# Infini-attention with a token-mixing MLP: packing the attention logits into 46 steps of seven PSUM banks

## The chip, the cores and the metric

The kernel runs on one core of a Trainium2 chip. The time is device time in microseconds (us), the median of several executions. TensorE (PE) does the matmuls into PSUM, which has eight banks of 512 fp32 columns in each of 128 partitions; ScalarE (ACT), VectorE (DVE) and GpSimd (POOL) work on what comes out of them; the queue of SyncE (SP) issues all DMAs. [...]

## The reference, cut to what matters

x has 2048 tokens of width 1024; there are 32 heads of width 32 and 4 segments of 512 tokens.

```python
xn = layernorm(x)
q, k, v = heads of xn @ wq, xn @ wk, xn @ wv          # (32 heads, 4 segments, 512, 32)
for s in range(4):
    logits = qs @ ks.T * 32 ** -0.5 + causal mask     # 512 x 512 for each head
    a_dot = softmax(logits) @ vs
    a_mem = (phi(qs) @ M) / (phi(qs) @ z + 1e-6)      # memory of the earlier segments
    o = g * a_mem + (1 - g) * a_dot                   # g = sigmoid(beta), by head
    M, z = M + phi(ks).T @ vs, z + sum(phi(ks))
h = layernorm(xn)
y = (gelu(h.T @ w1 + b1) @ w2 + b2).T                 # mixes tokens; 3584 hidden units
return x + concat(o) @ wo + y
```

phi(t) is t + 1 where t > 0 and exp(t) otherwise.

## The kernel before

**Stages.** In the first stage x is loaded and normalised, and the MLP's hidden layer is computed (`norm_and_first_hidden`, `hidden`): 896 matmuls of 512 columns into `gT`. In the second stage (`attention_and_out`) the attention runs, and between its parts stand the matmuls of the MLP's second layer with `w2h` and those of the output projection with `wo_sb`, which together are called the fill (`_Fill`). The last part of the output projection comes in `tail`.

**Units.** A unit is one segment of four heads: 32 units, numbered u = 8 x segment + group. Its q and k projections (`proj_q`, `proj_k`, eight matmuls each) give qT and kT, in which head r of the group holds partitions 32r to 32r + 31. Three buffers of each are in rotation, by u modulo 3. Two units make a pair p: A is unit 2p, B is unit 2p + 1.

**Logits.** A block (kb, r) of a unit is the product of head r's keys 128 kb to 128 kb + 127 with its queries from 128 kb to 511; queries before that are masked anyway. So it has 512, 384, 256 or 128 columns for kb = 0, 1, 2, 3. Its contraction runs over 32 rows, and `tile_position` puts it on row group r of TensorE's array, a strip of 32 rows. Blocks share banks: kb 1 with kb 3 of the same unit and head (384 + 128), kb 2 of A with kb 2 of B (256 + 256), and kb 0 alone. A pair thus fills 20 banks. `window` computes them in three windows of 7, 7 and 6 banks, of 10, 12 and 10 matmuls; the order in a window is a table, where A13 means unit A, kb 1, head 3:

```python
    WINDOWS = (
        "A00 A01 A02 A03 A10 A11 A12 A30 A31 A32",
        "A20 A21 A22 A13 B20 B21 B22 A33 B00 B01 A23 B23",
        "B10 B11 B02 B03 B30 B31 B12 B13 B32 B33",
    )
```

ACT takes the exp of each bank into one of 14 slots of `pT` (512 columns of bf16 each; `EXPS` and `place` fix which), and POOL zeroes the upper triangle of each diagonal block of 128 columns with an `affine_select`; `MASKS` groups these over slots, so that there are 11 selects for a pair.

**Products.** `weigh(u, qb)` multiplies the exps of the four heads, for 128 queries, with V (1280 matmuls of 33 columns in all), adds the memory's product with `pqT` and `MZbf` from the second segment on, and for qb = 3 the update with `pk`. `combine` divides and gates on DVE into `o_s`, and a transposing DMA puts that into `oT`.

**The order.** A planner in the program (`_Flow`) writes the order of all engines while the kernel is built. It keeps a modelled clock for each engine. TensorE's attention tasks wait in a list (`crit`); the planner takes one when its inputs and banks are ready in the model by 120 ns, otherwise it issues a fill matmul. `GOALS` says for each pair how many of the 1088 fill matmuls should be done by then, so the fill lasts until the end. A window or step is a `wall`: no task behind it is taken ahead of it. On the chip nothing is decided any more; the order stands. A window is priced in the model at 637 ns.

**Loads.** SP's queue issues the weights of wq and wk (two buffers each), the w2h blocks of seven matmuls (six buffers, two blocks ahead), x for the residual into one of three `stg` buffers, in which DVE adds the fill's result (line 1349), and the stores from there. At the end `tail` loads what was stored into `fin`, adds and stores it (line 1265).

Matmuls are recorded at line 217 and DMAs at line 245, both helpers'; exps of logits are line 1083, the selects line 1091, evictions of projections lines 987 and 988.

## Time and profile before

| | |
|---|---|
| median of 6 runs | 694.37 us (694.13 to 694.7) |
| the profiled execution's own time | 694.46 us |
| its span, first to last instruction | 692.5 us |
| TensorE (PE) busy | 688.0 us (99%), 4822 matmuls |
| ScalarE (ACT) busy | 281.9 us (41%), 513 instructions |
| VectorE (DVE) busy | 268.6 us (39%), 603 instructions |
| GpSimd (POOL) busy | 118.0 us (17%), 235 instructions |
| granted TensorE clock | 1.0 |
| DMA engines, mean over the span | 112 GB/s |

A busy share counts the time in which at least one instruction of the engine is under way. Matmuls overlap, and each is recorded with its way through the array and out, so a 512-column matmul shows 0.38 us although the next one starts earlier; the step from one start to the next is what it costs. PEld is the weight load, which runs beside the matmuls. In the timeline a row is a run of like instructions: start, length, engine, line, operation, output<-inputs, shape, count. In the chain of waits a row is start, length and what the end of the kernel was waiting for in that time.

### The profile page before, as it was taken

To read this page: it belongs to the slowest core of one execution; us is meant where nothing else is said; L and a number is where in the kernel's file an instruction comes from. 1 tells how busy PE (TensorE), PEld (TensorE's weight loads), DVE (VectorE), ACT (ScalarE), POOL (GpSimd) and SP (SyncE) were. 2 spreads that over 40 slices of the span, in tenths; PEclk is the share of its full clock that TensorE was granted. 3 is DMA by queue.
4 is the path that set the end of the run, shared out by engine and by line. 5 is a ranking of instruction groups with operands and counts; after the bars stand their busy time and mean duration, and the time that the engine had idled before them with its cause. 6 is when DMAs were issued, how large, how long until landed. Compare 5 with 4: busy or idle time off the path is not lost.

```text
span 692.5 us, 11588 instructions
## 1 busy us (share of the span) xinstructions
PE 688.0 (99%) x4822; PEld 329.0 (48%) x4822; DVE 268.6 (39%) x603; ACT 281.9 (41%) x513; POOL 118.0 (17%) x235
## 2 busy tenths in 40 slices
PE   8999999999999999999999999999999999999998
PEld 3444444444444544545445454444445454444544
DVE  6731100000002433434555464655556463453545
ACT  7431111111136364454544525354543525443450
POOL 4820000000001221221202112121212212121230
PEclk9999999999999999999999999999999999999999
DMA  8377666223038445446262643526263442424114
GB/s 306 122 183 181 153 157 212 88 61 101 1 106 186 103 94 133 103 109 137 46 147 63 134 96 81 124 52 147 53 145 82 94 110 53 116 57 117 38 26 147
DMA packets 211342, 77.32 MB, mean 112 GB/s; under 512 B 173915, under 2 KB 203611, under 8 KB 211291
## 3 DMA queue, kind: packets, MB, share of 16 engines
q1 hardware_dynamic: 211290, 76.59, 44.6%
q8 instruction: 38, 0.62, 0.4%
q14 instruction: 14, 0.11, 0.0%
HBM read 59.79 MB, written 5.24 MB: 94 GB/s over the span
## 4 chain that ended last, share of the span: by engine, by line
PE 98%; ACT 1%; DMA 0%; DVE 0%; POOL 0%; issue 0%; SPq 0%; DVEq 0%
PE ps_all L217 98%; ACT xn_tmp L806 0%; DMA xin<-in_A_x_dram 0%; ACT xn_tmp L808 0%; DVE h L847 0%; POOL ln_r L839 0%; SPq L245 0%; DVE fin L1265 0%; POOL ln_t L837 0%; DVE ln_mv L822 0%; DVEq L65 0%
## 5 line engine op out<-in xcount | busy, mean ns | idle before, releaser
L217 PE MATMUL ps_all<-gT,w2h 128*128 128x512 bf16 x896 | 229.0, 379 | 0.0
L1083 ACT ACTIVATE pT<-ps_all 128x512 bf16<-128x512 f32 x320 | 161.9, 617 | 111.3 <-PE ps_all L217 111.3
L217 PE MATMUL ps_all<-h,w1all 128*128 128x512 bf16 x896 | 193.9, 379 | 0.8 <-DVE h L847 0.6
L1091 POOL TENSOR_SCALAR_AFFINE_SELECT pT<-pT 128x256 bf16<-128x256 bf16 (+3 forms) x176 | 91.8, 527 | 544.3 <-ACT pT L1083 540.3
L217 PEld LDWEIGHTS ps_all<-h,w1all 128*128 128x128 bf16 x896 | 87.5, 98 | 107.2 <-issue 1.3
L217 PEld LDWEIGHTS ps_all<-gT,w2h 128*128 128x128 bf16 x896 | 79.9, 97 | 82.6 <-issue 7.8
L961 ACT ACTIVATE gT<-ps_all,bc 128x512 bf16<-128x512 f32 x56 | 37.7, 689 | 139.9 <-PE ps_all L217 139.9
L1129 DVE CAST ost<-ps_all 128x264 bf16<-128x264 f32 (+1 forms) x128 | 50.5, 397 | 80.4 <-PE ps_all L217 79.8
L217 PEld LDWEIGHTS ps_all<-vA,pT 128*128 128x128 bf16 x1280 | 50.3, 96 | 29.6 <-POOL pT L1091 0.5
L217 PE MATMUL ps_all<-xnT,wq 128*128 128x512 bf16 x256 | 60.5, 379 | 0.0
L217 PE MATMUL ps_all<-xnT,wk 128*128 128x512 bf16 x256 | 60.5, 379 | 0.0
L217 PE MATMUL ps_all<-wv_sb,xnT 128*128 128x512 bf16 x256 | 60.1, 379 | 0.0
L217 PE MATMUL ps_all<-vA,pT 128*128 128x33 bf16 x1280 | 51.7, 178 | 0.0
L988 DVE CAST qT<-ps_all 128x512 bf16<-128x512 f32 x29 | 20.1, 692 | 79.8 <-PE ps_all L217 79.8
L987 ACT ACTIVATE vA<-ps_all 128x512 bf16<-128x512 f32 x18 | 10.8, 599 | 90.6 <-PE ps_all L217 90.6
L899 DVE TENSOR_SCALAR gcol<-gcol 128x32 f32<-128x32 f32 x1 | 0.2, 181 | 118.5 <-ACT gcol L897 118.5
L217 PEld LDWEIGHTS ps_all<-wv_sb,xnT 128*128 128x128 bf16 x256 | 25.1, 98 | 30.2
L217 PEld LDWEIGHTS ps_all<-xnT,wk 128*128 128x128 bf16 x256 | 25.0, 98 | 30.2
L217 PEld LDWEIGHTS ps_all<-xnT,wq 128*128 128x128 bf16 x256 | 25.0, 98 | 30.1 <-issue 0.2
L987 ACT ACTIVATE kT<-ps_all 128x512 bf16<-128x512 f32 x32 | 19.1, 597 | 37.6 <-PE ps_all L217 37.6
L217 PE MATMUL ps_all<-wo_sb,oT 128*128 128x512 bf16 x128 | 34.3, 379 | 0.0
L972 DVE TENSOR_SCALAR etmp<-etmp 128x512 bf16<-128x512 bf16 x48 | 17.6, 367 | 39.0 <-ACT etmp L971 39.0
(68 smaller groups left out, 424.2 us busy)
## 6 DMA issues: line engine op xcount, KB each, us to landing
w2h<-in_B_w_dram SPq DMA_DIRECT2D x64, 224.0 KB, 3.3
w1all<-in_B_w_dram SPq DMA_DIRECT2D x12, 1024.0 KB, 5.3
wq<-in_A_wq_dram SPq DMA_DIRECT2D x32, 256.0 KB, 3.0
wk<-in_A_wk_dram SPq DMA_DIRECT2D x32, 256.0 KB, 2.9
stg<-in_A_x_dram SPq DMA_DIRECT2D x16, 256.0 KB, 3.6
out_dram<-stg SPq DMA_DIRECT2D x16, 256.0 KB, 3.1
xin<-in_A_x_dram SPq DMA_DIRECT2D x5, 512.0 KB, 7.3
wv_sb<-in_A_wv_dram SPq DMA_DIRECT2D x2, 1024.0 KB, 8.3
```

Source lines behind the costliest of these rows:

```text
L217: ins = self.nc.tensor.matmul(out, *args, **kwargs)
L899: fw.op("dve", lambda e: e.tensor_scalar(self.gcol[:], self.gcol[:], 1.0, None, op0=ALU.add), reads=[self.R_gcol], writes=[self.R_gcol])
L961: fw.op("act", lambda e: e.activation(self.gT[:, fc, half * 512:(half + 1) * 512], self.bank(b), ACT.Gelu_apprx_tanh, bias=self.b1c[:, fc: ...
L972: fl.op({"dve": (lambda e: e.tensor_scalar(et[:], et[:], 1.0, None, op0=ALU.min), 294, 330)}, [R_et], [R_et], prio=2)
L987: self.flow.op({"act": (lambda e, b: e.activation(dst, view(self.bank(b)), ACT.Copy), 635, 560), "dve": (lambda e, b: e.tensor_copy(dst, v ...
L988: "dve": (lambda e, b: e.tensor_copy(dst, view(self.bank(b))), 690, 727)},
L1083: fl.op({"act": (lambda e, b, slot=slot: e.activation(pT[:, slot, :], self.bank(b), ACT.Exp, scale=SCALE), 620, 530)}, [], [R[slot]], box= ...
L1091: fl.op({"pool": (lambda e, ap=ap, pat=pat: e.affine_select(ap, ap, pattern=pat, compare_op=ALU.is_ge, fill=0.0, base=0, channel_multiplie ...
L1129: fl.op({"dve": (lambda e, b: e.tensor_copy(dst, self.ps[:, b, 0:n * VW]), 150 + n * 35, 185 + n * 35)}, [], [self.R_ost[o][qb]], box=box, ...
```

## The change

The windows become steps. `logit_steps` lays the banks of each row group in one queue over all pairs: kb 0 of the first unit, its kb 1 with kb 3, kb 2 of both units, kb 0 of the second unit, its kb 1 with kb 3. A step takes one bank from each row group and a second bank from three of them; the one that is left out rotates (3, 2, 1, 0). That makes 45 steps of seven banks and a last one of five. `step` writes the matmuls bank by bank in that order. Each bank has its own slot of `pT`, taken from a free list of 18 and given back when the units in it have been weighed, and its own `affine_select` of one or two blocks, 320 in all. The loop of `attention_and_out` issues projections when a step two ahead needs them and weighs a unit once its last step is issued; the goals of the fill come from straight lines between points instead of the table. Beside that, `prod` becomes half as large (`combine` writes one half into `o_s` and adds the other), `etmp` has one buffer instead of two, `stg` two instead of three, and `o_s` moves to another place.

```diff
-    GOALS = (0, 0, 60, 119, 179, 238, 310, 382, 454, 526, 598, 670, 742, 814, 885, 956, 1026, 1085)
+    N_SLOT = 18
+    RESERVE = 60
...
-        self.prod = e.take("prod", [P, 32, D_HEAD], BF16)
-        self.R_prod = [Res(f"prod{k}", wait) for k in range(2)]
+        self.prod = e.take("prod", [P, 4, P], BF16)
+        self.R_prod = Res("prod", wait)
+        self.o_s = [e.take(f"o_s{i}", [P, 4, P], BF16) for i in range(2)]
+        self.R_os = [Res(f"o_s{i}", wait) for i in range(2)]
...
-        self.etmp = [e.take(f"etmp{i}", [P, SEG_L], BF16) for i in range(2)]
+        self.etmp = e.take("etmp", [P, SEG_L], BF16)
...
-        self.pT = e.take("pT", [P, 14, 512], BF16)
+        self.pT = e.take("pT", [P, self.N_SLOT, 512], BF16)
...
-        self.stg = [e.take(f"stg{i}", [P, D_MODEL], BF16) for i in range(3)]
+        self.stg = [e.take(f"stg{i}", [P, D_MODEL], BF16) for i in range(2)]
...
+        self.slots = deque(range(self.N_SLOT))
+        self.slot_of, self.users = {}, {}
...
-    def phi(self, dst, R_dst, src, R_src, k):
+    def phi(self, dst, R_dst, src, R_src):
 
         fl = self.flow
-        et, R_et = self.etmp[k], self.R_etmp[k]
+        et, R_et = self.etmp, self.R_etmp
...
-    def place(o, kb, qb, r):
-
-        j = qb - kb
-        if kb == 2:
-            return 8 + r, o * 256 + j * P
-        if o == 0:
-            return (r if kb == 0 else 4 + r), (384 if kb == 3 else j * P)
-        if kb == 0:
-            return (12 + r if r < 2 else r), j * P
-        return 4 + r, (384 if kb == 3 else j * P)
-
-    WINDOWS = (
-        "A00 A01 A02 A03 A10 A11 A12 A30 A31 A32",
-        "A20 A21 A22 A13 B20 B21 B22 A33 B00 B01 A23 B23",
-        "B10 B11 B02 B03 B30 B31 B12 B13 B32 B33",
-    )
-    EXPS = ((0, 1, 2, 3, 4, 5, 6), (7, 8, 9, 10, 11, 12, 13), (4, 5, 2, 3, 6, 7))
-    MASKS = (
-        ((0, 16, 4), (16, 28, 4), (19, 28, 4)),
-        ((28, 32, 3), (32, 48, 2), (48, 56, 4)),
-        ((16, 24, 4), (19, 24, 4), (8, 16, 4), (24, 32, 4), (27, 32, 4)),
-    )
-
-    def window(self, p, w):
+    def logit_steps():
+
+        todo = []
+        for r in range(4):
+            q = deque()
+            for p in range(N_UNIT // 2):
+                x, y = 2 * p, 2 * p + 1
+                for blocks in (((x, 0),), ((x, 1), (x, 3)), ((x, 2), (y, 2)), ((y, 0),), ((y, 1), (y, 3))):
+                    q.append((r, blocks))
+            todo.append(q)
+        steps = []
+        while any(todo):
+            n = len(steps)
+            take = [q.popleft() for q in todo if q]
+            for r in range(4):
+                if todo[r] and r != (3 - n) % 4:
+                    take.append(todo[r].popleft())
+            steps.append(take)
+        return steps
+
+    def step(self, items):
         fl = self.flow
-        slots = self.EXPS[w]
-        items = [("AB".index(t[0]), int(t[1]), int(t[2])) for t in self.WINDOWS[w].split()]
-        units = sorted({2 * p + o for o, _, _ in items})
-        reads = [R[u % 3] for u in units for R in (self.R_kT, self.R_qT)]
+        slots, jobs, reads = [], [], []
+        for r, blocks in items:
+            slot = self.slots.popleft()
+            slots.append(slot)
+            col, masks = 0, []
+            for u, kb in blocks:
+                self.slot_of[u, r, kb] = (slot, col)
+                jobs.append((len(slots) - 1, u, r, kb, col))
+                masks.append(col // P)
+                col += SEG_L - kb * P
+                for R in (self.R_kT[u % 3], self.R_qT[u % 3]):
+                    if R not in reads:
+                        reads.append(R)
+            self.users[slot] = {u for u, _ in blocks}
+            items[len(slots) - 1] = (r, blocks, slot, masks)
 
         def mms(*bs):
-            bank = dict(zip(slots, bs))
-            for o, kb, r in items:
-                k = (2 * p + o) % 3
-                slot, col = self.place(o, kb, kb, r)
-                n_q = SEG_L - kb * P
-                self.fw.mm(self.ps[:, bank[slot], col:col + n_q],
-                           self.kT[k][32 * r:32 * r + 32, kb * P:(kb + 1) * P],
-                           self.qT[k][32 * r:32 * r + 32, kb * P:SEG_L],
+            for i, u, r, kb, col in jobs:
+                self.fw.mm(self.ps[:, bs[i], col:col + SEG_L - kb * P],
+                           self.kT[u % 3][32 * r:32 * r + 32, kb * P:(kb + 1) * P],
+                           self.qT[u % 3][32 * r:32 * r + 32, kb * P:SEG_L],
                            start=True, stop=True, tile_position=(32 * r, 0))
 
         box = fl.pe(mms, reads, banks=len(slots), wall=True, ns=637)
         pT, R = self.pT, self.R_pT
-        for i, slot in enumerate(slots):
+        for i, (r, blocks, slot, masks) in enumerate(items):
             fl.op({"act": (lambda e, b, slot=slot: e.activation(pT[:, slot, :], self.bank(b), ACT.Exp, scale=SCALE),
                            620, 530)}, [], [R[slot]], box=box[i], give=True)
-        v = pT[:].rearrange("p a (j q) -> p (a j) q", q=P)
-        for b0, b1, st in self.MASKS[w]:
-            ap = v[:, b0:b1:st, :]
-            rs = [R[i] for i in sorted({x // 4 for x in range(b0, b1, st)})]
-            pat = [[0, ap.shape[1]], [1, P]]
-            ns = 180 + 115 * ap.shape[1]
+            v = pT[:, slot, :].rearrange("p (j q) -> p j q", q=P)
+            if len(masks) > 1:
+                ap, pat = v[:, masks[0]:masks[1] + 1:masks[1] - masks[0], :], [[0, 2], [1, P]]
+            else:
+                ap, pat = v[:, masks[0], :], [[1, P]]
+            ns = 180 + 115 * len(masks)
             fl.op({"pool": (lambda e, ap=ap, pat=pat: e.affine_select(ap, ap, pattern=pat, compare_op=ALU.is_ge,
                                                                       fill=0.0, base=0, channel_multiplier=-1),
-                            ns, ns + 30)}, rs, rs)
+                            ns, ns + 30)}, [R[slot]], [R[slot]])
...
-        where = {(r, kb): self.place(u % 2, kb, qb, r) for r in range(4) for kb in range(qb + 1)}
+        where = {}
+        for r in range(4):
+            for kb in range(qb + 1):
+                slot, col = self.slot_of[u, r, kb]
+                where[r, kb] = slot, col + (qb - kb) * P
...
-            for k in range(2):
+            for k, to, R_to in ((0, os, R_os), (1, self.prod, self.R_prod)):
                 v = ost[:].rearrange("p (q k r) x -> p q k r x", q=4, k=2)[:, :, k, :, 0:D_HEAD]
                 rk = rec.rearrange("p (q k r) -> p q k r", q=4, k=2)[:, :, k, :].unsqueeze(3)
-                pk = self.prod[:].rearrange("p (k q r) d -> p k q r d", q=4, k=2)[:, k]
+                pk = to[:].rearrange("p q (r d) -> p q r d", d=D_HEAD)
                 dve(lambda e, v=v, rk=rk, pk=pk: e.tensor_tensor(pk, v, rk.to_broadcast([P, 4, 4, D_HEAD]), op=ALU.mult),
-                    R_ost + [R_rec], [self.R_prod[k]], 640)
-            pv = self.prod[:].rearrange("p (k q r) d -> p k q (r d)", q=4, k=2)
-            dve(lambda e: e.tensor_tensor(os[:], pv[:, 0], pv[:, 1], op=ALU.add), self.R_prod, [R_os], 424)
+                    R_ost + [R_rec], [R_to], 640)
+            dve(lambda e: e.tensor_tensor(os[:], os[:], self.prod[:], op=ALU.add), [R_os, self.R_prod], [R_os], 424)
...
-        for p in range(N_UNIT // 2):
-            a, b = 2 * p, 2 * p + 1
-            fl.stage = p + 1
-            self.window(p, 0)
-            self.proj_q(a + 2)
-            self.proj_k(a + 2)
-            self.window(p, 1)
-            self.proj_v(a)
-            for qb in range(4):
-                self.weigh(a, qb)
-            self.combine(a)
-            self.window(p, 2)
-            self.proj_q(b + 2)
-            self.proj_k(b + 2)
-            for qb in range(4):
-                self.weigh(b, qb)
-            self.combine(b)
-            self.proj_v(b)
-        self.stall = fl.run(self.GOALS)
+        steps = self.logit_steps()
+        first, last = {}, {}
+        for i, items in enumerate(steps):
+            for _, blocks in items:
+                for u, _ in blocks:
+                    first.setdefault(u, i)
+                    last[u] = i
+        made, u = 2, 0
+        for i, items in enumerate(steps):
+            fl.stage = i + 1
+            self.step(items)
+            while True:
+                if made < N_UNIT and made < u + 3 and first[made] <= i + 2:
+                    self.proj_q(made)
+                    self.proj_k(made)
+                    made += 1
+                elif u < N_UNIT and last[u] <= i:
+                    self.proj_v(u)
+                    for qb in range(4):
+                        self.weigh(u, qb)
+                    self.combine(u)
+                    for slot in [x for x, us in self.users.items() if u in us]:
+                        self.users[slot].discard(u)
+                        if not self.users[slot]:
+                            del self.users[slot]
+                            self.slots.append(slot)
+                    u += 1
+                else:
+                    break
+        goals = [0, 0]
+        knots = [(0, 0)] + [(last[8 * s + 7] + 2, 245 + 288 * s) for s in range(3)]
+        knots += [(len(steps) - 1, self.fill.total - self.RESERVE), (len(steps), self.fill.total - 3)]
+        for i in range(1, len(steps) + 1):
+            (x0, y0), (x1, y1) = next((k0, k1) for k0, k1 in zip(knots, knots[1:]) if k0[0] <= i <= k1[0])
+            goals.append(y0 + (y1 - y0) * (i - x0) / (x1 - x0))
+        self.stall = fl.run(goals)
...
-                self.flow.dma(lambda: fw.dma(k.stg[m % 3][:], k.x_d[:, k.mlp_order[m], :], writes=[k.R_stg[m % 3]]),
-                              [], [k.R_stg[m % 3]]) if m < len(k.mlp_order) else None
+                self.flow.dma(lambda: fw.dma(k.stg[m % 2][:], k.x_d[:, k.mlp_order[m], :], writes=[k.R_stg[m % 2]]),
+                              [], [k.R_stg[m % 2]]) if m < len(k.mlp_order) else None
...
-            m = j % 3
+            m = j % 2
```

## The prediction

> **What bounds the kernel now.** I read the page first, then the chain of work that ended last, then the waits, then the timeline of TensorE around the instructions that the change touches.

> ```profile
> PE 688.0 (99%) x4822; PEld 329.0 (48%) x4822; DVE 268.6 (39%) x603; ACT 281.9 (41%) x513; POOL 118.0 (17%) x235
> ```

> TensorE is busy for 688.0 of 692.5 us, all others under half. Busy matmuls overlap, so that alone proves little. The chain of waits does:

> ```profile
> 12.38 660.89 PE ps_all L217 x4597
> 673.31 16.77 PE ps_all L217 x123
> 690.11 0.36 DVE fin L1265
> ```

> From 12.38 us to 690 us the chain is TensorE alone; the one break, before 673.31, is a wait of 0.2 us for the last masks. So no wait is left to win and any cover is nearly whole: time changes by what TensorE's own stream gains or loses, plus new waits. The timeline prices that stream:

> ```profile
> 322.60 1.89 PE L217 MATMUL ps_all<-wv_sb,xnT 128*128 128x512 bf16 x8
> 324.32 1.24 PE L217 MATMUL ps_all<-gT,w2h 128*128 128x512 bf16 x5
> 325.50 0.61 PE L217 MATMUL ps_all<-qT,kT 32*128 32x512 bf16 x10
> 326.04 1.25 PE L217 MATMUL ps_all<-gT,w2h 128*128 128x512 bf16 x5
> 327.13 1.89 PE L217 MATMUL ps_all<-xnT,wq 128*128 128x512 bf16 x8
> 328.86 0.59 PE L217 MATMUL ps_all<-gT,w2h 128*128 128x512 bf16 x2
> ```

> Take differences of starts, not durations. Eight full matmuls last 324.32 - 322.60 = 1.72 us, or 0.216 us each for 512 columns: 0.054 us for 128 columns, which I call one unit. The logits window lasts 326.04 - 325.50 = 0.54 us; the other two kinds of window, in the same view,

> ```profile
> 306.81 0.62 PE L217 MATMUL ps_all<-qT,kT 32*128 32x256 bf16 x12
> 307.36 1.25 PE L217 MATMUL ps_all<-gT,w2h 128*128 128x512 bf16 x5
> ...
> 313.02 0.61 PE L217 MATMUL ps_all<-qT,kT 32*128 32x384 bf16 x10
> 313.57 0.39 PE L217 MATMUL ps_all<-gT,w2h 128*128 128x512 bf16 x1
> ```

> last 0.55 us each. A window's matmuls use 32 rows, so four run side by side, one in each row group. The fullest row group of each window takes 1024 columns, 8 units or 0.43 us; 0.11 us is left for leaving the mode. Entering costs too: five full matmuls take 325.50 - 324.32 = 1.18 us where 5 x 0.216 = 1.08 would do, so 0.10 us. The view of the logits' matmuls alone, by stretches of that window, shows the side by side:

> ```profile
> 325.49:325.71 0.22, 0.21 (x4) 1.00 0.30 39
> 325.72:325.88 0.16, 0.16 (x7) 1.00 1.29 267
> ```

> For 0.22 us only four matmuls are there, one per row group; the fifth in order, for row group 0 again, appears once the first has streamed its 512 columns. A matmul whose row group is taken waits.

> **The change, part by part.**

> *Steps in place of windows.* The matmuls of the logits are the same 512, and all other matmuls keep their count in the built program (4,822). 48 windows become 46 steps. Column sums: each row group has 16 x 20 units of work, and the steps give no row group more than 8 units, so with perfect packing 46 x 8 = 368 units stand against 48 x 8 = 384. That is -16 x 0.054 = -0.86 us, and two entries and exits fewer are -2 x 0.21 = -0.42 us.

> But the order inside changes as well. A window was written group by group: 384 columns for row groups 0, 1, 2, and only then the 128 that share their banks. `step` writes bank by bank: a slot with blocks 1 and 3 gives 384 and then 128 columns to the *same* row group, next to each other; a slot of two blocks 2 gives 256 and 256. The second of a pair must wait for the first, by the stretch view above. What do the matmuls behind it do, which are for idle row groups? In the windows of before this never comes up: I walked all three by hand, and each matmul's row group comes free no later than its turn, so both answers give 8 units. The row that is nearest shows a wait but not what stands behind one.

> [...] I work out both.

> In order: a matmul starts at the later of (its row group free, the previous matmul's start). Example, the 13th step: row groups 0 to 3 with 3+1 units each, then 0 to 2 with 2+2. Group 0: 3 units at 0, 1 unit at 3. Group 1 can start only at 3: 3 units, then 1 at 6. Group 2 at 6, its 1 at 9. Group 3 at 9, its 1 at 12. Then group 0 takes 2 at 12 and 2 at 14, group 1 at 14 and 16, group 2 at 16 and 18: the end is 20 units, not 8. The pattern of slots repeats after 20 steps; their lengths in units are 14, 14, 17, 17, 12, 17, 17, 12, 16, 17, 11, 14, 20, 14, 13, 19, 14, 14, 16, 17, sum 305. 46 steps are two rounds and the first six again (the last step has five banks, also 17): 2 x 305 + 91 = 701 units. Against 384 units: +317 x 0.054 = +17.1 us. With the two entries and exits: +16.7 us.

> Independently: 368 units, -0.86 - 0.42 = -1.3 us.

> I take the first. [...]

> *Masks.* 176 selects become 320, one per slot: 192 of 256 columns and 128 of 128.

> ```profile
> L1091 POOL TENSOR_SCALAR_AFFINE_SELECT pT<-pT 128x256 bf16<-128x256 bf16 x112 | 48.1, 431 | 142.6 <-ACT pT L1083 139.7
> L1091 POOL TENSOR_SCALAR_AFFINE_SELECT pT<-pT 128x384 bf16<-128x384 bf16 x32 | 16.7, 522 | 14.4 <-ACT pT L1083 13.3
> ```

> A block of 128 costs 522 - 431 = 0.09 us more, so one alone is about 0.34 us. 192 x 0.431 + 128 x 0.34 = 126 us of POOL instead of 91.8, of a span of 690. What counts is the step: seven exps of a window take 3.54 us in the ACT timeline, 0.51 us apart, and a select takes 0.34 to 0.43, so POOL keeps up and ends less than 0.5 us after the last exp. The full matmuls that stand on TensorE between a step and the products that read it hide this; without that cover each step would pay up to 0.4 us, 46 x 0.4 = 18 us. From below, not grouping selects may remove the 0.2 us wait at 673, since the last step is now followed by 14 full matmuls (3.0 us). I take -0.2.

> *Exps, projections, combine.* 320 exps as before. Nine qT evictions move from DVE to ACT and six of vA the other way (692 ns and 597 ns for 512 columns): both engines stay under half busy, nothing. `combine` has the same number of operations; the sum now waits for `prod` and `o_s` as before. One `etmp` for two, so the k side's exp waits for the q side's last DVE pass, at most 0.63 + 0.37 + 0.70 us; pqT and pk are read by products that come at least a projection and many full matmuls later. Nothing; without cover, 24 times up to 1 us.

> *Slots and queue.* 18 slots only loosen waits. Two staging buffers instead of three: the load of a chunk of x now waits on SP's queue for the store of the previous chunk, and w2h, wq and wk loads stand behind it. Store to landing is 3.1 us. In the built order a w2h load and mostly a transpose of o_s, which waits for DVE, stand between store and load, and each chunk lasts about 30 us, so I take nothing. Upper end: 14 chunks x 3.1 us held, 43 us; unlikely.

> *Sum.* The profiled execution took 694.46 us (span 692.5), within 0.1 of the median 694.37. 694.4 + 17.1 - 0.4 - 0.2 = 710.9, said as 711.

> **Rivals.** (1) *Row groups run on independently*: a row group can hold the waiting half without stopping the queue. Even one waiting matmul per row group brings every step down to 8 units. Then 694.4 - 1.3 - 0.2 = 692.9 us, on the other side of no change. [...] The point of decision is whether group 1's 384 columns start beside group 0's 384 or with its 128. (2) *Weight loads add to it*: where a 54 ns block is followed by its row group's next one, that load (92 ns in the trace) is not covered; in the windows it was, and the measured 0.11 us exit leaves no room for more. At 46 steps x up to 0.1 us: 716 us. (3) *The products wait for masks or w2h*, with row groups independent: 692.9 plus about 0.2 us in each step, 702 us. Against: TensorE's chain has one wait today, and POOL is paced by ACT.

> **How the numbers follow.** In order, alone or with (2): 0.84. Independent: 0.13; at -1.5 us it lies on the edge of what a measurement of this kernel can tell (0.2%, 1.4 us), so I split it 0.07 faster and 0.06 the same. Waits (3): 0.03, slower. Slower is 0.84 + 0.03 = 0.87. The time is that of the in-order case. The range 704 to 716 holds that case with the fixed cost per step off by 0.1 us either way (46 x 0.1 = 4.6 us) and some half steps overlapping; that is about 0.8, so it need not reach the faster case.

> **What would show it.** Right: steps of 0.7 to 1.2 us from first logits matmul to the next full one, mean about 15.2 x 0.054 + 0.11 = 0.93 us, the longest every 20th from the 13th; TensorE still one unbroken chain; other rows at the same 0.216 us. Wrong by (1): every step 0.55 us. Wrong by (3): PEld or PE rows that wait for POOL's pT or for w2h.

## The result and the profile after

The changed kernel takes 692.93 us (median of 19 runs, 692.78 to 693.19) against 694.43 us for the old one in the same comparison: the ratio is 0.9978, with a 95% interval of 0.9972 to 0.9984. It is faster by 1.5 us, where the prediction said slower by 17 and left the time of its rival (1), 692.9 us, outside its range.

The page of the changed kernel, first row of engines:

```profile
PE 686.7 (99%) x4822; PEld 329.4 (48%) x4822; DVE 260.5 (38%) x600; ACT 284.0 (41%) x516; POOL 145.8 (21%) x379
```

TensorE has lost 1.3 us and is still the bound. The chain of waits, its last pieces (start, length, what):

```profile
12.39 676.43 PE ps_all L217 x4703
688.84 0.36 DVE fin L1292
```

The chain is now TensorE without any break from 12.39 us to the end: the wait of 0.2 us for the last masks, before 673.31 us in the old kernel, is gone, and nothing new has come. The first stage, which was not changed, takes the same time: the first fill matmul starts at 214.41 us in the old trace and at 214.42 in the new one. So the difference of the spans, 692.474 - 691.215 = 1.26 us, lies in TensorE's own stream behind that point. The times differ by 1.50 us. The other 0.24 us or so lies outside the spans, before the first or after the last instruction (694.46 - 692.47 = 1.99 us in the old kernel's profiled execution, 692.94 - 691.22 = 1.72 in the new one's); no run here explains it.

Here is the 13th step, for which the prediction worked out 20 units (1.08 us, and 0.11 us more at its end), in the timeline of TensorE:

```profile
322.02 1.46 PE L217 MATMUL ps_all<-gT,w2h 128*128 128x512 bf16 x6
323.41 0.62 PE L217 MATMUL ps_all<-qT,kT 32*128 32x384 bf16 x14
323.96 1.25 PE L217 MATMUL ps_all<-gT,w2h 128*128 128x512 bf16 x5
```

It lasts 323.96 - 323.41 = 0.55 us, like an old window, and so do all others: the 45 full steps and the last one take 541 to 559 ns by the starts in the trace, the 48 old windows 541 to 549. The view of the logits' matmuls alone, in stretches of that step (stretch, its length, PE's busy time, the number of matmuls that touch it; the last three figures, clock and DMA, play no part here), says how:

```profile
323.40:323.57 0.17, 0.16 (x4) 1.00 1.12 337
323.58:323.63 0.05, 0.05 (x8) 1.00 1.08 246
323.64:323.74 0.10, 0.10 (x11) 1.00 0.78 184
```

The program has 384, 128, 384, 128, 384, 128, 384, 128 columns here, for row groups 0, 0, 1, 1, 2, 2, 3, 3. In the first 0.17 us four matmuls are under way; the single starts in the trace are 4, 11, 17 and 24 ns after the step's first weight load, all 384 columns wide. The second instruction in the program, 128 columns for row group 0, starts at 177 ns. So three later instructions started ahead of it. That was the point of decision which the prediction named, and it fell the other way. It also corrects a sentence that stands at the beginning, that on the chip nothing is decided any more and the order stands: between row groups, TensorE's starts in this trace do not keep the order of the program (11, 17 and 24 ns ahead of 177).

### The profile page after: what moved, and what is told of

The parts are those of the page before. It is cut to its first block, busy times and chain, and to the rows that moved or that the text cites. A ratio compares the mean times of both kernels' runs of the same rounds, so it can differ in the third digit from the quotient of the medians.

```text
span 691.2 us, 11771 instructions
## 1 busy us (share of the span) xinstructions
PE 686.7 (99%) x4822; PEld 329.4 (48%) x4822; DVE 260.5 (38%) x600; ACT 284.0 (41%) x516; POOL 145.8 (21%) x379
## 4 chain that ended last, share of the span: by engine, by line
PE 98%; ACT 1%; DMA 0%; DVE 0%; POOL 0%; issue 0%; SPq 0%; DVEq 0%
PE ps_all L217 98%; ACT xn_tmp L809 0%; DMA xin<-in_A_x_dram 0%; ACT xn_tmp L811 0%; DVE h L850 0%; POOL ln_r L842 0%; SPq L245 0%; DVE fin L1292 0%; POOL ln_t L840 0%; DVE ln_mv L825 0%; DVEq L65 0%
## 5 line engine op out<-in xcount | busy, mean ns | idle before, releaser
L217 PE MATMUL ps_all<-gT,w2h 128*128 128x512 bf16 x896 | 228.5, 379 | 0.0
L1098 POOL TENSOR_SCALAR_AFFINE_SELECT pT<-pT 128x256 bf16<-128x256 bf16 (+1 forms) x320 | 119.4, 375 | 506.1 <-ACT pT L1090 493.5
L217 PE MATMUL ps_all<-h,w1all 128*128 128x512 bf16 x896 | 193.9, 379 | 0.8 <-DVE h L850 0.7
L217 PEld LDWEIGHTS ps_all<-h,w1all 128*128 128x128 bf16 x896 | 87.4, 98 | 107.3 <-DMA w1all<-in_B_w_dram 1.0
L217 PEld LDWEIGHTS ps_all<-gT,w2h 128*128 128x128 bf16 x896 | 79.8, 97 | 85.2 <-issue 10.3
L217 PEld LDWEIGHTS ps_all<-vA,pT 128*128 128x128 bf16 x1280 | 50.3, 96 | 28.7
L217 PE MATMUL ps_all<-xnT,wq 128*128 128x512 bf16 x256 | 60.5, 379 | 0.0
L217 PE MATMUL ps_all<-xnT,wk 128*128 128x512 bf16 x256 | 60.5, 379 | 0.0
L217 PE MATMUL ps_all<-wv_sb,xnT 128*128 128x512 bf16 x256 | 60.1, 379 | 0.0
L217 PE MATMUL ps_all<-vA,pT 128*128 128x33 bf16 x1280 | 51.5, 178 | 0.0
L217 PEld LDWEIGHTS ps_all<-wv_sb,xnT 128*128 128x128 bf16 x256 | 25.1, 98 | 30.2
L217 PEld LDWEIGHTS ps_all<-xnT,wk 128*128 128x128 bf16 x256 | 25.1, 98 | 30.2
L217 PEld LDWEIGHTS ps_all<-xnT,wq 128*128 128x128 bf16 x256 | 25.1, 98 | 30.2
L975 DVE TENSOR_SCALAR etmp<-etmp 128x512 bf16<-128x512 bf16 x48 | 14.1, 294 | 61.3 <-ACT etmp L974 61.3
L991 DVE CAST vA<-ps_all 128x512 bf16<-128x512 f32 x20 | 13.9, 694 | 56.7 <-PE ps_all L217 54.2
L217 PE MATMUL ps_all<-wo_sb,oT 128*128 128x512 bf16 x128 | 33.1, 379 | 0.0
L991 DVE CAST qT<-ps_all 128x512 bf16<-128x512 f32 x20 | 13.8, 692 | 46.1 <-PE ps_all L217 46.1
```

Of the source, the lines that this page charges most:

```text
L217: ins = self.nc.tensor.matmul(out, *args, **kwargs)
L975: fl.op({"dve": (lambda e: e.tensor_scalar(et[:], et[:], 1.0, None, op0=ALU.min), 294, 330)}, [R_et], [R_et], prio=2)
L991: "dve": (lambda e, b: e.tensor_copy(dst, view(self.bank(b))), 690, 727)},
L1098: fl.op({"pool": (lambda e, ap=ap, pat=pat: e.affine_select(ap, ap, pattern=pat, compare_op=ALU.is_ge, fill=0.0, base=0, channel_multiplie ...
```

## The experiments

Two questions were open. How far does TensorE look past a waiting matmul: (A) a matmul whose row group is taken waits without stopping the queue, however many wait, or (B) a row group holds some small number of waiting matmuls, and the next one stops the queue? And where did the gain come from: (C) from the smaller number of steps, or (D) from better waits? In the expectations, N is the number of matmuls that a row group can hold, the running one included. The queue was tested first, by order alone: the work of a step stays the same, only the list changes.

**All of one row group together.** In `step`, ahead of `mms`:

```diff
+        work = [sum(it[0] == r for it in items) for r in range(4)]
+        jobs.sort(key=lambda j: (work[j[2]], j[2]))
```

> The changed kernel with the matmuls of a step sorted by row group, so that all of one row group (three in most steps, four in 13 of them) stand together, the row group with one bank first. Unit: 128 columns, 0.054 us. Theory A (a waiting matmul does not stop the queue, however many wait): every step stays 8 units long, 0.55 us, time 692.9 us. Rival B (each row group holds one running and one waiting matmul, the next one stops the queue): 671 units instead of 368, +16.4 us, 709 us. Rival C (one running and two waiting): 416 units, +2.6 us, 695.5 us. In-order queue as in the prediction: 954 units, +32 us, 725 us.

Measured: 693.49 us (693.37 to 693.81), ratio to the old kernel 0.9986 (0.9977 to 0.9995). The 13th step in its timeline:

```profile
323.57 0.64 PE L217 MATMUL ps_all<-qT,kT 32*128 32x384 bf16 x14
324.14 1.25 PE L217 MATMUL ps_all<-gT,w2h 128*128 128x512 bf16 x5
```

324.14 - 323.57 = 0.57 us with four matmuls of a row group in a row. One waiting matmul per row group (709 us) and two (695.5 us) are both out, and so is the in-order queue (725 us). The mean step, from the starts in the trace, is 562.3 ns against 550.5: 46 x 11.8 ns = 0.54 us, close to the 0.56 us between the two medians (whose intervals overlap). Single starts show where it goes: in the fourth step the four row groups begin at 4, 11, 21 and 31 ns, with one, two and two waiting matmuls passed over between them, where the old windows begin at 3 to 4 ns intervals. Passing over a waiting matmul cost some 3 ns here (7, 10 and 10 ns from one of these starts to the next, against 3 to 4), not the length of a matmul (54 ns for 128 columns). In the 13th step the last row group begins at 37 ns, behind seven waiting matmuls of the other three.

**In the order in which row groups come free.**

```diff
+        at, due = [0] * 4, []
+        for j in jobs:
+            due.append((at[j[2]], len(due), j))
+            at[j[2]] += SEG_L - j[3] * P
+        jobs[:] = [x[2] for x in sorted(due)]
```

> The changed kernel with the matmuls of a step in the order in which their row groups come free (first blocks of all row groups, then the second ones), as the windows of the old kernel had it. The in-order queue of the prediction: no matmul would stand behind a waiting one any more, so 701 units go to 368, 18 us faster than the changed kernel. Theory A: the order is nearly free; the mean step of 550.5 ns goes to the 545.2 ns of the old windows, 46 x 5.3 ns = 0.24 us, 692.7 us.

Measured: 692.69 us (692.49 to 693.27), 0.9975 (0.9965 to 0.9985), as A has it. The mean step is 545.0 ns, the old windows' 545.2. In its timeline the 13th step is 324.11 - 323.57 = 0.54 us:

```profile
323.57 0.61 PE L217 MATMUL ps_all<-qT,kT 32*128 32x384 bf16 x14
324.11 1.25 PE L217 MATMUL ps_all<-gT,w2h 128*128 128x512 bf16 x5
```

This is the lowest median here; the 0.24 us between it and the changed kernel is what the steps in its trace account for (46 x 5.5 ns = 0.25 us), though the intervals overlap. Three orders of the same matmuls give three lengths (562.3, 550.5 and 545.0 ns a step), so the order in the program makes a difference.

**Eight in a row, and its control.** Each matmul is cut into pieces of 128 columns, 28 in a step. One kernel puts the eight pieces of a row group together, the other takes one piece of each row group in turn:

```diff
+        parts = [(i, u, r, kb, q, col + (q - kb) * P) for i, u, r, kb, col in jobs for q in range(kb, 4)]
...
-                self.fw.mm(self.ps[:, bs[i], col:col + SEG_L - kb * P],
+                self.fw.mm(self.ps[:, bs[i], col:col + P],
...
-                           self.qT[u % 3][32 * r:32 * r + 32, kb * P:SEG_L],
+                           self.qT[u % 3][32 * r:32 * r + 32, q * P:(q + 1) * P],
```

> The changed kernel with each logits matmul cut into pieces of 128 columns, sorted by row group: eight pieces of one row group stand together, 28 matmuls and 28 weight loads in a step. Theory A with a deep queue: no longer than the same pieces in order of columns (the run beside it). If a row group can hold N matmuls, running one included, a step is 8 units for N of 8 or more, 10 for 7, 12 for 6, 14 for 5, 16 for 4, and 25 in order: 46 x 2 x 0.054 = +5.0 us for each one that N falls short of 8.

> Control: the same 128-column pieces, ordered by columns, row group after row group, so that no matmul ever waits behind another row group. Both theories: 8 units a step if the extra weight loads are hidden, 692.9 us; if each piece costs its 92 ns load instead of 54 ns of streaming, 8 x 38 ns x 46 = +14 us, 707 us. What the row-group order costs beyond this is the queue's.

Measured: 715.53 us (1.0303, 1.0288 to 1.0319) by row group, 693.65 us (0.9986, 0.9977 to 0.9995) in turns. A step each, in the timeline by row group,

```profile
329.34 1.11 PE L217 MATMUL ps_all<-qT,kT 32*128 32x128 bf16 x28
330.38 0.60 PE L217 MATMUL ps_all<-gT,w2h 128*128 128x512 bf16 x2
```

and in turns:

```profile
323.88 0.62 PE L217 MATMUL ps_all<-qT,kT 32*128 32x128 bf16 x28
324.44 1.25 PE L217 MATMUL ps_all<-gT,w2h 128*128 128x512 bf16 x5
```

1.04 us against 0.56. So A, without a limit, falls, and 0.56 us with 28 weight loads says that the loads are hidden: at the 92 ns that one takes in the traces of the old and the changed kernel, 28 in a row would be 2.58 us. (The control takes 0.72 us more than the changed kernel: 46 x 7.5 ns = 0.35 us in the steps, and in its trace the first stage, which no edit touches, ends 0.38 us later.) The 21.9 us between the two runs are 4.4 of the 5.0 us per missing place, so N would be 8 - 4.4 = 3.6. The single starts of the step shown, in ns, give a whole number. Behind the four pieces of the short row group, the next one's eight pieces start at 17, 84, 140, 195, 251, 307, 363 and 419 ns, and the first of the row group after it at 260 ns, right behind the fifth; the last row group's first starts at 502, behind the fifth of its predecessor at 494. With the fifth running, three were still waiting. For N = 4 the expectation has 16 units. The step takes 1045 ns; without the 0.11 us at its end that is some 935 ns, or 16 pieces of 56 ns, which is what one costs here, and 40 ns more. A queue that looks past three waiting matmuls altogether would do the same here, though the seven of the first order speak against it, so two more orders were run.

**Turns of four, turns of five.** From the control, the sorting key only:

```diff
-            due.append((at[j[2]], work[j[2]], len(due), j))
+            due.append((at[j[2]] // 4, work[j[2]], j[2], len(due), j))
```

and // 5 in the other.

> The 128-column pieces again, in turns of four: four pieces of one row group, four of the next, and so on. Theory N = 4 (each row group holds one running and three waiting matmuls): nothing stops, 8 units a step, within 0.6 us of the pieces by columns (693.7 us). Rival (the queue as a whole looks past three waiting matmuls, which fits the run with eight in a row as well): 11 units a step, 506 instead of 368 in all, +7.5 us, 701 us.

> The 128-column pieces in turns of five. Theory N = 4: the fifth of a turn stops the queue for one unit, 458 units instead of 368, 10 units a step, +4.9 us over the pieces by columns, 698.5 us. N = 5 or more: no change, 693.9 us. The queue as a whole looking past three waiting ones: 551 units, +9.9 us, 703.5 us.

Measured: 694.81 us (1.0005, 0.9996 to 1.0014) and 700.2 us (1.0084, 1.007 to 1.0098). The logits' matmuls at the beginning of a step, in turns of four,

```profile
323.84:323.90 0.06, 0.05 (x4) 1.00 0.87 307
```

and in turns of five:

```profile
325.55:325.61 0.06, 0.05 (x2) 1.00 0.73 273
325.62:325.66 0.04, 0.04 (x5) 1.00 1.63 461
```

With four in a row, all four row groups have begun within 0.06 us, behind three, six and nine waiting matmuls: the limit belongs to the row group, not to the queue. With five in a row, the third row group begins only once the second piece of its predecessor has started (93 ns, behind 85). A step takes 594 ns with four and 710 with five: 116 ns more, two units as N = 4 has it. Both times missed their expectations for N = 4. Four in a row was 1.2 us over the control where at most 0.6 was expected: by the steps it is 46 x 36 ns = 1.6 us (594 against 558), mostly because the four row groups begin 13 ns apart, the last of them 44 ns after the step's first weight load; the first stage, which no edit touches, ends 0.45 us earlier in this trace than in the control's. Five in a row was 6.6 us over the control where 4.9 was expected: by the steps it is 6.9 us, the same 1.6 us and 5.3 us for the two units. In these runs a row group, then, held one running and three waiting matmuls, and only the fifth in a row stopped the queue (710 ns a step against 594). Whether the limit counts matmuls, or weight loads with them, was not tried, nor five in a row with more than 128 columns each.

**More steps.** `logit_steps` takes a second bank from two row groups instead of three:

```diff
-                if todo[r] and r != (3 - n) % 4:
+                if todo[r] and len(take) < 6 and (r - n) % 4 < 2:
```

> The changed kernel with six banks in a step instead of seven (two row groups get a second bank, rotating): 54 steps, 53 of them again 8 units deep, the last 4. Theory (time follows the number of steps): each further step costs 8 units and one entry and exit, 0.43 + 0.21 = 0.65 us, so 7.5 x 0.65 = +4.9 us over the changed kernel, 697.8 us. Rival (the gain came from better waits, not from two fewer steps): smaller steps release the exps earlier, so the time stays within 0.5 us of 692.9.

Measured: 698.5 us (1.0059, 1.0046 to 1.0073), 5.6 us over the changed kernel. C holds, D falls. From the traces, whose spans differ by 5.55 us: the logits' stretches, exits included, sum to 29.36 us instead of 25.33 (+4.03); eight entries more are 8 x 0.105 = +0.84 (the last full matmul ahead of a step takes 312 ns to the next start instead of 216, and the first full matmul behind it 226); and the rest is two new waits and the first stage. The chain shows the waits, which were not expected:

```profile
10.05 0.73 DVE h L850 x2
12.60 533.18 PE ps_all L217 x3527
545.82 111.38 PE ps_all L217 x892
657.22 0.60 ACT pT L1090
657.88 2.62 POOL pT L1098 x4
660.54 33.83 PE ps_all L217 x243
```

There is a break at 545.82 us, and at the end TensorE waits for ACT's exp and POOL's masks: 0.20 and 0.24 us lost. The long run began at 12.60 instead of 12.39 us.

**Only the last wait.** The old kernel with other goals:

```diff
-    GOALS = (0, 0, 60, 119, 179, 238, 310, 382, 454, 526, 598, 670, 742, 814, 885, 956, 1026, 1085)
+    GOALS = (0, 0, 60, 119, 179, 238, 310, 382, 454, 526, 590, 660, 730, 800, 868, 936, 1002, 1060)
```

> The old kernel with only its last table of goals changed (590, 660, 730, 800, 868, 936, 1002, 1060 in place of the last eight), which keeps 25 full matmuls instead of 1 for the end, 13 of them between the last window and the first product behind it. Theory: the wait of 0.2 us for the last masks goes and nothing else, 694.2 us; 48 windows still last 545 ns. Rival (the changed order of the end is worth more than the wait): below 693.8 us.

Measured: 694.31 us (694.18 to 694.49), 0.9999 (0.9989 to 1.0008): the same. The edit missed what it was for. The chain of waits has its break elsewhere:

```profile
1.25 666.73 PE ps_all L217 x4611
667.98 0.03 issue
668.01 21.95 PE ps_all L217 x147
```

The break of 0.19 us, before 668.01 us, is the old one at the old place in the program: ahead of the last unit's first products, behind 19 full matmuls since the last window, as many as before. The edit only put 24 more behind those products (147 matmuls in the last piece instead of 123). So this run does not say what the wait is worth; it only says that another order of the end gains nothing by itself (694.31 us against 694.40 in the same comparison). Where the wait comes from can be read in the timelines of the end. In the old kernel,

```profile
667.64 0.61 PE L217 MATMUL ps_all<-qT,kT 32*128 32x384 bf16 x10
669.41 0.56 PE L217 MATMUL ps_all<-vA,pT 128*128 128x33 bf16 x16
670.07 3.04 ACT L1083 ACTIVATE pT<-ps_all 128x512 bf16<-128x512 f32 x6 [2.76 <-PE ps_all L217]
671.22 3.05 POOL L1091 TENSOR_SCALAR_AFFINE_SELECT pT<-pT 128x256 bf16<-128x256 bf16 x5 [3.37 <-ACT pT L1083]
```

and in the changed one:

```profile
660.04 0.62 PE L217 MATMUL ps_all<-qT,kT 32*128 32x384 bf16 x9
660.70 2.56 ACT L1090 ACTIVATE pT<-ps_all 128x512 bf16<-128x512 f32 x5 [2.89 <-PE ps_all L217]
661.37 2.37 POOL L1098 TENSOR_SCALAR_AFFINE_SELECT pT<-pT 128x256 bf16<-128x256 bf16 x5 [3.19 <-ACT pT L1090]
```

The exps of the old last window start 670.07 - 667.64 = 2.43 us behind it, when the last products of the unit before are through: they write slots 2 to 7 of `pT`, which those products read. With 18 slots from the free list they start 0.66 us behind it, so the masks are done in time although only 14 full matmuls stand there. That this ended the wait is read from the two traces; it was not isolated.

## Why the prediction was wrong, point by point

- **What bounds the kernel**: right. TensorE's chain has one break of 0.2 us in the old kernel and none in the new one, and its stream explains the difference of the spans.
- **Steps in place of windows, the packing**: the prediction's -0.86 us for the columns and -0.42 us for two entries and exits were near. Measured in the traces: 48 stretches of 545.2 ns are 26.17 us, 46 of 550.5 ns are 25.33 us, so -0.85. This holds two exits less, and also 46 x 5.3 ns = +0.24 us which the steps lose by their order, a term that the sum for independent row groups had at nothing. Two entries less are another -0.21. With the lost wait: -0.85 - 0.21 - 0.20 = -1.26 us, the difference of the spans.
- **Steps in place of windows, the order inside**: this is the step that failed. "I take the first", it said: the queue waits behind the second half of a bank, 701 units instead of 368. The runs showed 368: a row group held three waiting matmuls (594 ns a step with four in a row, 710 with five), and a list written bank by bank needs room for one. No run shows the +17.1 us of the sum; in its place the steps measure +0.24 us, 550.5 instead of 545.2 ns a step, where about 930 were forecast. The working of the 701 units is right for a queue without any place to wait; that TensorE's is one was an assumption, which no row of the trace of before shows. The trace of the changed kernel has a start at 11 ns ahead of one at 177 that precedes it in the program.
- **How the ends were weighed**: no window of the old kernel put a matmul for a free row group behind a waiting one; the prediction said so, and yet gave the in-order case 0.84. That was its author's estimate; the trace of before showed neither case. It had worked out that one waiting place per row group is enough for 692.9 us, and gave this 0.13. That its 692.9 us for that case is also the time measured is in part luck: the 0.24 us for the order that it left out and the 0.24 us or so outside the spans, which nobody forecast, cancel.
- **Masks**: right that they hide, and that the wait of 0.2 us ends; but it gave the 14 full matmuls behind the last step as the reason, and the old kernel had 19 there. The timelines of the end point to the exps, which no longer wait for slots. 320 selects cost 80.5 + 39.1 = 119.6 us against 126 estimated, in the groups by shape; one block alone takes 307 ns, not 340:

```profile
L1098 POOL TENSOR_SCALAR_AFFINE_SELECT pT<-pT 128x256 bf16<-128x256 bf16 x192 | 80.5, 421 | 202.8 <-ACT pT L1090 193.3
L1098 POOL TENSOR_SCALAR_AFFINE_SELECT pT<-pT 128x128 bf16<-128x128 bf16 x128 | 39.1, 307 | 303.4 <-ACT pT L1090 300.2
```

- **Exps, projections, two staging buffers**: nothing, as said; no wait for any of them stands in TensorE's chain. With that rival (3) falls, too. The slots, also taken as nothing, probably gave the 0.2 us.
- **Rival (2)**, weight loads between short blocks: it falls, by the control with 28 loads in 0.56 us.

## What to carry to other kernels

On a kernel whose chain of waits is one engine from end to end, count what that engine does: here a step less saves 0.65 us (0.545 for the step, 0.105 for the full matmuls on both sides of it), and of the rest of a large rewrite only a lost wait of 0.2 us and 0.24 us for the order showed in the trace. Matmuls on separate row groups hardly needed to be interleaved by hand here (0.24 us of 693), as long as no more than four in a row went to the same one (694.81 us with pieces in turns of four, 700.2 us in turns of five). And when two assumptions give results on opposite sides of zero and the trace of before never exercises the case, it speaks for neither: keep both ends in the range, or find an instruction that would tell them apart.
